# A transformer block, forward and backward, on one core: q and k of two chunks turned token-major by DMA, the first chunk's FFN in two token halves, its residual added by TensorE, and a new order

## The chip, the core and the metric

The kernel runs on one core of a Trainium2 chip. What is measured is the device time of one execution in microseconds (us); each kernel is run several times and the median is used. Before the change the three runs took 554.25, 555.15 and 555.99 us, so the median is 555.15. Beside these there is one execution under the hardware profiler, from which every row in this text comes. Engines are named as in the profile: PE is TensorE's matmul stream, PEld its weight loads, DVE is VectorE, ACT is ScalarE, POOL is GpSimd, SP is SyncE, which here does nothing but issue DMAs.

## The reference

A pre-norm block with a local attention and an FFN; the kernel returns the block's output and, for a given grad_out, the gradients of x, wqkv, wo, w1, b1, w2 and b2. Batch 1, S = 2048 tokens, D = 512, F = 1792, 32 heads of 16, window of 8 with a step of 2 back in time; inputs and outputs are bf16.

```python
def _A_ref(x, wqkv, wo):
    B, S, D = x.shape
    H = 32; Dh = D // H
    W, dil = 8, 2
    qkv = (lambda x, *d: x.transpose(*d))((x @ wqkv).reshape(B, S, 3, H, Dh), 2, 0, 3, 1, 4)
    q, k, v = qkv[0], qkv[1], qkv[2]
    pos = jnp.arange(S)
    off = jnp.arange(W) * dil
    idx = pos[:, None] - off[None, :]
    ...
    logits = jnp.einsum("bhsd,bhswd->bhsw", q, kg) * scale
    logits = jnp.where(mask[None, None, :, :], logits, -1e9)
    attn = _softmax(logits, axis=-1)
    o = jnp.einsum("bhsw,bhswd->bhsd", attn, vg)
    return (lambda x, *d: x.transpose(*d))(o, 0, 2, 1, 3).reshape(B, S, D) @ wo

def _B_ref(x, w1, b1, w2, b2):
    h = jnp.einsum("bsd,df->bsf", x, w1) + b1
    h = _gelu(h)
    return jnp.einsum("bsf,fd->bsd", h, w2) + b2

x = A_x
h = x + _A_ref(_layernorm(x, axis=-1), A_wqkv, A_wo)
h2 = h + _B_ref(_layernorm(h, axis=-1), B_w1, B_b1, B_w2, B_b2)
return h2
```

The outputs are h2 and, by jax.vjp, the seven gradients.

## The kernel before

The tokens are worked on in four chunks of 512, each of four tiles of 128 tokens. Per chunk the forward pass has the first layernorm; q and k as feature-major tiles (kt, qt: features on partitions, tokens along them) and v as a token-major one (tokens on partitions); attention, whose windowed products VectorE makes (prf, prbo) and TensorE sums over features with a 0/1 matrix; the product with wo and the residual (h); the second layernorm; its transposed copy ln2T; the FFN's first product and the gelu; and the second product, which gives h2. The backward pass follows chunk by chunk, and then the weight gradients, which run over all tokens.

Nothing is issued as it is written down. Every step is an op of a plan (L84), with its engine and what it reads and writes; a hand-given table, ORDER, says in which order the ops are emitted (L118 to L156), and thereby the program order of each engine, and a second table, HOMES, gives each buffer its place in SBUF or PSUM. Each engine goes through its program strictly in order, so an instruction that waits holds up all that stand behind it. Most DMAs are issued by SP, in order too; the gathers of the window (L471, 2304 KB each) by POOL, and a few stores by ACT. DMAs take their semaphores from eight lanes in turn, and one that takes a lane waits until the DMA eight places before it has landed.

What the change touches:

- **Token-major k and q.** The backward pass gathers windows of k and q from DRAM, token-major (k_d, q_d). p1_qkv decides at its end how they get there. Before the change all four chunks use to_tm_store: for each half chunk eight PE transposes (L434), one eviction of 128x1024 by ACT into tmk or tmq (L297) and one store of 256 KB (L287). The functions fm_store and tm_late also exist, but the table TML that selects them is empty: the first stores the feature-major tile to DRAM (kf_d, qf_d), the second loads it back through a transposing DMA (L291) into tmlk or tmlq and stores that to k_d or q_d.
- **The residual.** p1_h makes the product with wo in a PSUM tile, four matmuls for each tile of 128 tokens, and VectorE adds x (xp) out of SBUF while evicting (L747). Then come BN_STATS and BN_AGGR for each tile, and in layernorm, for four tiles at a time, ve (L371), a power on POOL (L373) and nm (L376); ACT applies them (L381) into ln_0, and to_fm_tiles transposes ln_0 on PE (L416) and has ACT evict ln2T.
- **The FFN's first product.** p2_h makes 14 PSUM tiles per chunk, each four matmuls of 512 columns, ACT adds the bias while evicting (xb, L774), and a gelu follows for each group of up to four (L777).
- **mmul** (L264 to L270) issues a product whole (L270) or, where its neighbours in the order use 32-column groups, as four 32-column pieces (L268), which TensorE streams beside each other.

Other names that come up: w1T is w1 loaded by a transposing DMA for the backward FFN; ro, ln1b and gw1in are loads from DRAM for the weight gradients; wgs and wgso are evicted weight gradients and their stores; gqkvT is a transposed gradient copied by ACT.

Of the kernel before, what the change touches and what calls it, by code (L numbers as in the profile page):

```python
# [10 lines left out]
P = 128  # L11
BF16 = mybir.dt.bfloat16
F32 = mybir.dt.float32
ACT = mybir.ActivationFunctionType
# [145 lines left out]
def kernel(  # L160
# [568 lines left out]
    def p1_h(c):  # L729
# [5 lines left out]
        for j in range(TPC):  # L735
            ps = ps_("psw", 1)

            def mm(j=j, ps=ps):
                for k in range(DC):
                    mmul(ps(), oT()[:, j, k * P:(k + 1) * P], wo()[:, k, :], start=(k == 0), stop=(not RESPE and k == DC - 1))  # L740
                if RESPE:
                    T.matmul(ps(), lhsT=ident[:], rhs=xt()[:, j, :], start=False, stop=True)
            op("PE", (5 if RESPE else 4) * MM, mm, r=[(oT, None if c in FMO else j // 2), wo] + ([xt, IDENT] if RESPE else []), w=[ps], tag="wo", cls=4)
            if RESPE:
                evict(h, lambda j=j: h()[:, j, :], ps, lambda ps=ps: ps(), 512, key=j, tag="h")
            else:
                op("DVE", tt_us(512, True), lambda j=j, ps=ps: V.tensor_tensor(out=h()[:, j, :], in0=ps(), in1=xt()[:, j, :], op=ALU.add),  # L747
                   r=[ps, xt], w=[(h, j)], tag="h")
        ln2 = sb("ln2_%d" % c, [P, TPC, D])
        layernorm(c, h, MV2, ST2, VE2, NM2, R2, mv2, st2, ve2, nm2, rstd2, ln2, N2[c], "2")  # L750
# [8 lines left out]
    def p2_h(c):  # L759
        d = st_[c]  # L760
        d["g"], d["d"] = [], []
        for b, (f0, f1) in enumerate(FB):
            n = f1 - f0
            N = n * 512
            xb = sb("xb", [P, n, 512])
            gl = sb("gl", [P, n, 512])
            for f in range(f0, f1):
# [407 lines left out]
TML = ()  # L1175
# [3 lines left out]
RESPE = False  # L1179
# [150 lines left out]
```

## Time and profile before

| | |
|---|---|
| median of three runs | 555.15 us |
| the profiled execution's own time | 557.15 us |
| its span, first to last instruction | 555.4 us |
| granted TensorE clock, mean | 0.999 |
| bytes moved by DMA | 126.40 MB |
| idle gaps of PE in front of chunk 0's FFN, 62 to 76 us | 1.78 us in three waits |
| evictions L297 of tmk and tmq, 16 | 16.1 us of ACT |
| residual additions L747, 16 | 10.8 us of DVE |
| bias evictions L774, 56 | 35.7 us of ACT |

The profile's span is 1.75 us shorter than the execution's time, and the profiled execution is 2.0 us longer than the median of the runs. In the rows below, a group's row reads: line, engine, operation, output and input names, shape and type, count, then busy us and the mean ns of one, then the idle time of that engine just before and what ended it. In a timeline row the first number is the start in us from the span's start, the second the length; square brackets give the idle time before and what ended it. A slice's digit is the busy share in tenths.

### The profile page before, as it was taken

Reading aid. Unit: us, or ns where it says so; the run is one execution under the profiler, and the core shown is the slowest. Engines: PE = TensorE matmul, PEld = TensorE weight load, DVE = VectorE, ACT = ScalarE, POOL = GpSimd, SP = SyncE. Lnnn points to the kernel's source line nnn. Section 1 sums busy time; section 2 is a strip of 40 time slices with the busy share of each in tenths; the row PEclk is TensorE's granted clock in tenths of the full one; section 3 lists DMA queues with packets and bytes.
Section 4 is the critical chain, followed back from the end, with each engine's and each line's share of the span. In section 5 each row is a group of like instructions: output and inputs, shape, how many; then the busy total and the mean of one; then the engine's idle time right before and its main releaser. Section 6 shows DMA issues by size and latency. Waiting matters only on the chain. (4 is left out here: it accounts for less than half of the span.)

```text
span 555.4 us, 13067 instructions
## 1 busy us (share of the span) xinstructions
PE 539.7 (97%) x5568; PEld 268.9 (48%) x5568; DVE 494.2 (89%) x648; ACT 324.2 (58%) x503; POOL 32.4 (6%) x38
## 2 busy tenths in 40 slices
PE   7999999999999999999999999999999998999995
PEld 4655554444444444444444444455455554555442
DVE  7999999999999999889885877789879998999992
ACT  4998699887999794996131324042324556633531
POOL 1610100021001000000000000000010001000000
PEclk9999999999999999999999999999999999999999
DMA  8898998975499617298999989999999999778237
GB/s 265 218 289 251 395 368 236 199 228 185 97 268 281 179 34 167 77 152 221 199 210 184 194 183 187 295 212 271 240 357 374 305 335 372 318 272 162 52 72 199
DMA packets 195306, 126.40 MB, mean 228 GB/s; under 512 B 149744, under 2 KB 190896, under 8 KB 193200
## 3 DMA queue, kind: packets, MB, share of 16 engines
q1 hardware_dynamic: 189760, 82.06, 64.5%
q0 software_dynamic: 3312, 41.42, 19.2%
q10 hardware_dynamic: 2176, 2.10, 1.2%
q8 instruction: 43, 0.70, 0.5%
q14 instruction: 15, 0.12, 0.1%
HBM read 55.74 MB, written 35.21 MB: 164 GB/s over the span
## 5 line engine op out<-in xcount | busy, mean ns | idle before, releaser
L270 PE MATMUL ps<-goT,w2T 128*128 128x512 bf16 x224 | 53.6, 379 | 0.8 <-DVE h2s L828 0.5
L270 PE MATMUL ps<-w1T,xb 128*128 128x512 bf16 x224 | 52.9, 379 | 0.0
L270 PE MATMUL ps<-w,gl 128*128 128x512 bf16 x216 | 50.5, 379 | 0.0
L297 ACT CAST wgs<-ps 128x512 bf16<-128x512 f32 (+1 forms) x30 | 16.2, 558 | 57.4 <-PE ps L268 35.7
L270 PE MATMUL ps<-ln2T,w 128*128 128x512 bf16 x188 | 44.2, 379 | 0.7 <-DVE xb L856 0.3
L774 ACT ACTIVATE xb<-ps,b1c 128x512 bf16<-128x512 f32 x56 | 35.7, 692 | 12.8 <-PE ps L270 12.5
L856 DVE SCALAR_TENSOR_TENSOR xb<-xb,ps 128x512 bf16<-128x512 bf16 x56 | 36.6, 685 | 6.2 <-PE ps L270 5.6
L518 DVE TENSOR_TENSOR prbq<-Rq,cfq 128x4096 bf16<-128x4096 bf16 x16 | 36.0, 2288 | 5.0 <-PE ps L487 1.7
L479 DVE TENSOR_TENSOR prb<-got,vw 128x4096 bf16<-128x4096 bf16 x16 | 36.3, 2282 | 2.7 <-PE ps L487 1.4
L518 DVE TENSOR_TENSOR prbv<-Rv,cfv 128x4096 bf16<-128x4096 bf16 x16 | 36.1, 2283 | 2.7 <-PE ps L268 1.8
L518 DVE TENSOR_TENSOR prbk<-Rk,cfk 128x4096 bf16<-128x4096 bf16 x16 | 36.1, 2283 | 0.7 <-PE ps L527 0.7
L518 DVE TENSOR_TENSOR prbo<-Ro,cfo 128x4096 bf16<-128x4096 bf16 x16 | 35.9, 2288 | 0.4 <-DMA k_d<-tmk 0.2
L479 DVE TENSOR_TENSOR prf<-qt,kt 128x4096 bf16<-128x4096 bf16 x16 | 35.5, 2275 | 0.0
L270 PEld LDWEIGHTS <-w2T 128*128 128x128 bf16 x224 | 21.8, 98 | 27.4 <-issue 2.0
L270 PEld LDWEIGHTS <-xb 128*128 128x128 bf16 x224 | 21.9, 98 | 26.4
L270 PEld LDWEIGHTS <-gl 128*128 128x128 bf16 x216 | 20.8, 98 | 25.6 <-issue 1.6
L796 ACT ACTIVATE xb<-xb 128x2048 bf16<-128x2048 bf16 (+1 forms) x16 | 26.8, 1690 | 7.8 <-DVE xb L795 7.7
L626 PE MATMUL ps<-ln1T,wqk 128*32 128x512 bf16 x512 | 30.2, 383 | 0.0
L270 PEld LDWEIGHTS <-w 128*128 128x128 bf16 x188 | 18.1, 97 | 23.0 <-issue 2.5
L268 PE MATMUL ps<-wqkvT,gqkvT 128*32 128x512 bf16 x448 | 27.4, 379 | 1.7 <-ACT gqkvT L297 1.6
L777 ACT ACTIVATE gl<-xb 128x2048 bf16<-128x2048 bf16 (+1 forms) x16 | 26.8, 1697 | 0.0
L792 ACT ACTIVATE x<-xb 128x2048 bf16<-128x2048 bf16 (+1 forms) x16 | 26.6, 1690 | 0.0
(198 smaller groups left out, 1054.0 us busy)
## 6 DMA issues: line engine op xcount, KB each, us to landing
Ro<-v_d POOLq DMA_DIRECT2D x4, 2304.0 KB, 11.2
Rq<-k_d POOLq DMA_DIRECT2D x4, 2304.0 KB, 11.6
Rv<-go_d POOLq DMA_DIRECT2D x4, 2304.0 KB, 14.2
Rk<-q_d POOLq DMA_DIRECT2D x4, 2304.0 KB, 13.4
g_d<-gl SPq DMA_DIRECT2D x9, 512.0 KB, 3.5
gh_d<-xb SPq DMA_DIRECT2D x9, 512.0 KB, 3.4
w<-in_B_w_dram SPq DMA_DIRECT2D x2, 1792.0 KB, 15.0
out_dram<-wgs SPq DMA_DIRECT2D x13, 256.0 KB, 7.1
```

Of the source, the lines that this page charges most:

```text
L268: T.matmul(out[32 * a:32 * a + 32, :], lhsT=l[:, 32 * a:32 * a + 32], rhs=r, start=start, stop=stop, skip_group_check=True)
L270: T.matmul(out, lhsT=l, rhs=r, start=start, stop=stop, skip_group_check=True)
L297: fn = lambda: A.copy(out=ap(), in_=pap())
L479: op("DVE", tt_us(4096), lambda g=g, pr=pr: V.tensor_tensor(out=pr(), in0=ql()[:, g, :].unsqueeze(1).to_broadcast([P, W, 512]), in1=_sub(k ...
L518: V.tensor_tensor(out=pr().rearrange("p a j (d h) -> p a j d h", h=H), in0=_sub(R()[:, o0, 0:1], [[st, 2], [512, 4], [32, DH], [1, H]]), i ...
L626: T.matmul(ps()[32 * a:32 * a + 32, gg * 512:(gg + 1) * 512], lhsT=_sub(wq_()[:, dc, 0:1], [[DH, H]], sel * D + 4 * g + a), rhs=rhs, start ...
L774: op("ACT", act_us(512, 1), lambda f=f, ps=ps, xb=xb, f0=f0: A.activation(out=xb()[:, f - f0, :], in_=ps(), func=ACT.Identity, bias=b1c[:, ...
L777: op("ACT", act_us(N), lambda xb=xb, gl=gl: A.activation(out=fl(gl), in_=fl(xb), func=ACT.Gelu_apprx_tanh), r=[xb], w=[gl], tag="gelu", mo ...
L792: op("ACT", act_us(N), lambda xb=xb, x2=x2: A.activation(out=fl(x2), in_=fl(xb), func=ACT.Square), r=[xb], w=[x2], tag="x2")
L796: op("ACT", act_us(N), lambda xb=xb: A.activation(out=fl(xb), in_=fl(xb), func=ACT.Tanh, scale=GC), w=[xb], tag="tanh", mode=6)
L856: op("DVE", 0.61, lambda f=f, ps=ps, z=z, f0=f0: V.scalar_tensor_tensor(out=z()[:, f - f0, :], in0=z()[:, f - f0, :], scalar=1.0, in1=ps() ...
```

## The change

It does four things.

1. TML now names k and q of chunks 2 and 3. For these to_tm_store (16 transposes, two ACT copies and two stores each) is replaced by fm_store and tm_late: a 512 KB store, a 512 KB transposing load and a 512 KB store, all three issued by SP.
2. RESPE names chunk 0: its residual comes from one more matmul per tile, the identity against x, in the same PSUM accumulation, and ACT casts the sum into h (L297) where VectorE added it (L747).
3. HALVES names chunk 0: its FFN's first product runs over two halves of 256 tokens, each 14 groups of four matmuls of 256 columns and 14 bias evictions of 128x256; a half needs only two of the four tiles of ln2T. The second layernorm of that chunk takes its tiles in groups of two.
4. ORDER and HOMES are new throughout.

```diff
                 for k in range(DC):
-                    mmul(ps(), oT()[:, j, k * P:(k + 1) * P], wo()[:, k, :], start=(k == 0), stop=(not RESPE and k == DC - 1))
-                if RESPE:
-                    T.matmul(ps(), lhsT=ident[:], rhs=xt()[:, j, :], start=False, stop=True)
...
-            if RESPE:
+                    mmul(ps(), oT()[:, j, k * P:(k + 1) * P], wo()[:, k, :], start=(k == 0), stop=(c not in RESPE and k == DC - 1))
+                if c in RESPE:
+                    mmul(ps(), ident[:], xt()[:, j, :], start=False, stop=True)
...
+            if c in RESPE:
                 evict(h, lambda j=j: h()[:, j, :], ps, lambda ps=ps: ps(), 512, key=j, tag="h")
...
-        layernorm(c, h, MV2, ST2, VE2, NM2, R2, mv2, st2, ve2, nm2, rstd2, ln2, N2[c], "2")
+        layernorm(c, h, MV2, ST2, VE2, NM2, R2, mv2, st2, ve2, nm2, rstd2, ln2, N2[c], "2", per=2 if c in HALVES else TPC)
...
+        xbs = [sb("xb", [P, f1 - f0, 512]) for f0, f1 in FB] if c in HALVES else ()
+        for f, hh in [(f, hh) for hh in range(2) for f in range(FT)] if c in HALVES else ():
+            ps, xb, i, o = ps_("psi", 1), xbs[f // 4], f % 4, 256 * hh
+
+            def mmh(f=f, ps=ps, o=o):
+                for dc in range(DC):
+                    mmul(ps()[:, 0:256], w1()[:, dc, f * P:(f + 1) * P], cols(ln2T[c], dc, False)[:, o:o + 256], start=(dc == 0), stop=(dc == DC - 1))
+            op("PE", 4 * MM / 2, mmh, r=[w1, (ln2T[c], 2 * hh), (ln2T[c], 2 * hh + 1)], w=[ps], tag="ff1", cls=4)
+            op("ACT", act_us(256, 1), lambda f=f, ps=ps, xb=xb, i=i, o=o: A.activation(out=xb()[:, i, o:o + 256], in_=ps()[:, 0:256], func=ACT.Identity,
+                                                                                   bias=b1c[:, f:f + 1]), r=[ps, B1C], w=[(xb, (f, hh))], tag="xb")
...
-TML = ()
+TML = tuple((n, c) for n in "kq" for c in (2, 3))
...
-RESPE = False
+RESPE = (0,)
+HALVES = (0,)
...
 ORDER = (
-    8, 22, 0, 11, 12, 23, 1, 7, 10, 6, 9, 48, 364, 27, 13, 49, 50, 26, 51, 44, 61, 28, 2, 62, 40, 25, 3, 45, 29, 41, 24, 46, 52, 42, 43, 53, 363, 15,
+    8, 10, 0, 65, 6, 21, 12, 14, 7, 27, 48, 9, 26, 49, 15, 50, 25, 11, 19, 51, 18, 40, 28, 44, 41, 1, 2, 3, 4, 29, 5, 42, 43, 52, 45, 61, 36, 24, 17,
...
```

In the changed file the lines below p2_h lie ten further on (the bias eviction of the halves is L770, r_d's and rst's lines go from L1114 and L1117 to L1124 and L1127); the helpers' lines are the same.

How the new order moves instructions is shown at three places. The numbers within a name are those of one buffer, and say nothing else. First SP, from the transposing loads of normalised tiles (ln2T) to the loads of w1T; r_d, rst and xp are small loads and stores, g_d, gh_d and out_dram stores of results. Before:

```order
L291 DMA_TRANSPOSE ln2T_478_34_1913<-ln_2_465_34_1879 128x16x128
L287 DMA k_d<-tmk_23_538 128x2x512
L1114 DMA r_d<-rtr 16x32
L291 DMA_TRANSPOSE ln2T_533_38_2030<-ln_1_520_37_2003 128x16x128
L287 DMA g_d_73<-gl_27_1688 128x4x512
L1117 DMA rst<-r_d 32x4x16
L287 DMA out_dram<-h2s_35_1915 128x1x512
L1117 DMA rst<-r_d 32x4x16
L287 DMA gh_d_77<-xb_28_1394 128x4x512
L291 DMA_TRANSPOSE w1T_41_2268<-in_B_w_dram 128x14x128 x2
```

Now:

```order
L291 DMA_TRANSPOSE ln2T_535_39_2098<-ln_1_520_38_2067 128x16x128
L287 DMA g_d_73<-gl_31_1805 128x2x512
L291 DMA_TRANSPOSE tmlk_42_2121<-kf_d_91 128x4x512
L287 DMA q_d<-tmlq_32_1886 128x4x512
L287 DMA out_dram<-h2s_36_2034 128x1x512
L282 DMA xp_415_29_1702<-in_A_x_dram 32x4x512
L287 DMA k_d<-tmlk_42_2121 128x4x512
L291 DMA_TRANSPOSE tmlq_41_2240<-qf_d_86 128x4x512
L287 DMA q_d<-tmlq_41_2240 128x4x512
L287 DMA out_dram<-h2s_36_2034 128x1x512
L287 DMA g_d_73<-gl_32_1816 128x4x512
L1084 DMA k_d<-zrow 16x512
```

The next row there is the pair of w1T loads. Two transposing loads and three 512 KB stores of k and q have come in; the store of tmlq into q_d stands directly behind the load that fills tmlq, and w1T behind both.

Second, ACT from the last casts before chunk 0's FFN into that FFN. ln_0 and ln2T are the normalised tiles and their transposed copy, xb the bias evictions, ost the attention output of the next chunk. Before:

```order
L297 COPY ln2T_303_25_1293<-ps 128x4x128 x2
L297 CAST qt_293_20_1246<-ps 128x1024
L297 COPY tmk_28_1380<-ps 128x1024
L297 COPY tmk_29_1386<-ps 128x1024
L774 ACTIVATE xb_28_1394<-ps,b1c 128x512 x2
L532 ACTIVATE ost_27_1431<-ps 128x512 x2
L774 ACTIVATE xb_28_1460<-ps,b1c 128x512
L532 ACTIVATE ost_27_1431<-ps 128x512
L297 COPY tmq_29_1475<-ps 128x1024
L532 ACTIVATE ost_27_1431<-ps 128x512
L297 COPY oT_355_30_1493<-ps 128x1024
```

Now:

```order
L297 CAST qt_311_24_1375<-ps 128x1024
L532 ACTIVATE ost_29_1416<-ps 128x512
L297 COPY ln2T_314_26_1389<-ps 128x4x128 x2
L532 ACTIVATE ost_29_1416<-ps 128x512
L770 ACTIVATE xb_28_1450<-ps,b1c 128x256
L770 ACTIVATE xb_29_1456<-ps,b1c 128x256
L770 ACTIVATE xb_30_1466<-ps,b1c 128x256
L297 COPY oT_345_32_1474<-ps 128x1024
L770 ACTIVATE xb_30_1466<-ps,b1c 128x256
L532 ACTIVATE ost_29_1416<-ps 128x512
L770 ACTIVATE xb_29_1456<-ps,b1c 128x256 x2
```

The copies of tmk and tmq are gone from between the bias evictions, and these are of 256 columns.

Third, SP in the late stage, where the loads of ro and ln1b for the last weight gradients stand among the stores of wgs. Before:

```order
L282 DMA ro_1474_36_4943<-o_d_71 128x2048
L287 DMA out_dram<-wgs_1492_37_5032 128x2x512
L287 DMA out_dram<-wgs_1403_38_4568 128x2x256
L282 DMA ln1b_34_5284<-ln_d_62 32x4x512
L282 DMA ln1b_31_5422<-ln_d_64 32x4x512
L287 DMA out_dram<-wgs_1533_34_5360 128x2x512
L282 DMA ro_1556_32_5451<-o_d_72 128x2048
L282 DMA ln1b_33_5453<-ln_d_61 32x4x512
L282 DMA ln1b_31_5422<-ln_d_64 32x4x512
```

Now:

```order
L282 DMA ro_1483_41_5265<-o_d_71 128x2048
L287 DMA out_dram<-wgs_1363_41_4682 128x2x512
L287 DMA out_dram<-wgs_1418_42_4845 128x2x256
L287 DMA out_dram<-wgs_1366_39_4689 128x2x512
L287 DMA out_dram<-wgs_1462_40_5140 128x2x512
L287 DMA out_dram<-wgs_1510_40_5339 128x2x512
L282 DMA ln1b_32_5654<-ln_d_64 32x4x512
L282 DMA ln1b_34_5675<-ln_d_63 32x4x512 x2
```

Before, a ro load stood among the ln1b loads; now all ro loads stand ahead of the first of them, with five stores of wgs between.

More of the change, by code (lines that the diff above doesn't have):

```diff
@@ L739, in mm @@
                 for k in range(DC):
-                    mmul(ps(), oT()[:, j, k * P:(k + 1) * P], wo()[:, k, :], start=(k == 0), stop=(not RESPE and k == DC - 1))
-                if RESPE:
-                    T.matmul(ps(), lhsT=ident[:], rhs=xt()[:, j, :], start=False, stop=True)
-            op("PE", (5 if RESPE else 4) * MM, mm, r=[(oT, None if c in FMO else j // 2), wo] + ([xt, IDENT] if RESPE else []), w=[ps], tag="wo", cls=4)
-            if RESPE:
+                    mmul(ps(), oT()[:, j, k * P:(k + 1) * P], wo()[:, k, :], start=(k == 0), stop=(c not in RESPE and k == DC - 1))
+                if c in RESPE:
+                    mmul(ps(), ident[:], xt()[:, j, :], start=False, stop=True)
+            op("PE", (5 if c in RESPE else 4) * MM, mm, r=[(oT, None if c in FMO else j // 2), wo] + ([xt, IDENT] if c in RESPE else []), w=[ps], tag="wo", cls=4)
+            if c in RESPE:
                 evict(h, lambda j=j: h()[:, j, :], ps, lambda ps=ps: ps(), 512, key=j, tag="h")
@@ L764, in p2_h @@
             N = n * 512
-            xb = sb("xb", [P, n, 512])
+            xb = xbs[b] if c in HALVES else sb("xb", [P, n, 512])
             gl = sb("gl", [P, n, 512])
-            for f in range(f0, f1):
+            for f in range(f0, f1) if c not in HALVES else ():
                 ps = ps_("psh", 1)
```

203 rows, old and new, of tables (HOMES, ORDER) are left out of this document.

## The prediction

> **What bounds the kernel now.** I read the page's busy shares first, then its forty slices, then a table by stage, and only then single waits.
>
> ```profile
> PE 539.7 (97%) x5568; PEld 268.9 (48%) x5568; DVE 494.2 (89%) x648; ACT 324.2 (58%) x503; POOL 32.4 (6%) x38
> ```
>
> TensorE is busy 539.7 of 555.4 us: all idle time together is under 16 us, and by the slices, of 13.9 us each, a good part of that lies at the start and the end:
>
> ```profile
> PE   7999999999999999999999999999999998999995
> ...
> DVE  7999999999999999889885877789879998999992
> ...
> DMA  8898998975499617298999989999999999778237
> ```
>
> So the time is the matmul stream plus few gaps, and what leaves the stream is worth its full length wherever no other engine takes over as the bound. VectorE could: its digits are 9 from the second slice to the sixteenth, about 14 to 222 us, the stretch in which every edit of this change but the order lies. The table by 15 us shows how close the three engines are where the edits are:
>
> ```profile
> 60.00:75.00 15.00, 13.22 (x187) 7.77 (x185) 14.69 (x24) 11.19 (x14) 1.03 (x1) 1.00 1.00 392
> 75.00:90.00 15.00, 14.98 (x154) 8.16 (x153) 14.83 (x8) 14.39 (x23) 0.60 (x1) 1.00 0.91 286
> 90.00:105.00 15.00, 14.39 (x186) 6.69 (x185) 14.65 (x12) 14.24 (x16) 0.00 (x0) 1.00 0.86 242
> ```
>
> The columns are start and end, length, busy us of PE, PEld, DVE, ACT and POOL, granted clock, DMA share and GB/s. From 75 to 105 us PE has 29.4 of 30 us, DVE 29.5 and ACT 28.6: whoever gets more work there decides. The granted clock is 1.00 in each of these, so no term below is scaled by it.
>
> **TensorE's sum.** Four pairs (k and q of chunks 2 and 3) lose their 16 transposes each.
>
> ```profile
> 76.61 1.12 PE L434 MATMUL ps<-ident,kt 128*128 128x128 bf16 x16
> 77.61 2.75 PE L270 MATMUL ps<-ln2T,w 128*128 128x512 bf16 x12
> ```
>
> The next group starts 1.00 us after the 16 transposes of L434 began, so a group of 16 is worth 1.00 us of the stream and the four pairs 4.0 us. Other eights stand in the chain at 0.45 us, which would make it 3.6. I take 3.8. The residual of chunk 0 adds one identity matmul of 512 columns to each of four products:
>
> ```profile
> 477.15 0.86 PE ps L270 x4
> ```
>
> 0.86 us for four, so +0.9. The halves make 112 matmuls of 256 columns of 56 of 512. Two timeline rows give the spacing of 256 columns, one chain row that of 512 in the four-column-group form, and one row how fast its weights load:
>
> ```profile
> 371.37 2.78 PE L270 MATMUL ps<-gw1in,ln 128*128 128x256 bf16 x24
> 373.99 0.60 PE L270 MATMUL ps<-xw1in,ln 128*128 128x256 bf16 x4
> ```
> ```profile
> 422.30 2.59 PE ps L268 x48
> ```
> ```profile
> 455.08 0.12 PEld L527 LDWEIGHTS <-S 128*32 128x32 bf16 x8
> ```
>
> 24 take 2.62 us, 109 ns each against 0.86/4 = 215 ns for 512 columns: two halves cost 3 ns more than a whole, 0.2 us over 56 pairs. The built program issues 20 of the 112 in the form of four 32-column pieces. At 512 columns a piece takes 2.59/48 = 54 ns, and no row shows it at 256: 27 ns if the stream rules, 54 if the issue does, so +0 to +2.2 us over 80 pieces. Eight 32-column weight loads in 0.12 us say that four of them fit into 107 ns, so I take 0 and keep 2.2 for the range. Sum of TensorE: −3.8 + 0.9 + 0.2 = **−2.7 us**.
>
> The Trainium skill, "TensorE: Matmul & The Clock Gate", section "Back-to-back issue gap", speaks against the halves: it gives about 131 ns a matmul sustained at 512 columns and 81 ns at 128. By it (98 ns at 256 columns by a straight line, an estimate from that page) a pair of halves would cost 64 ns more than a whole and the 56 pairs 3.6 us, and the sum would be +0.7 instead of −2.7. The rows above, 109 ns against 215, speak against it.
>
> **VectorE**, which must fall too if TensorE's gain is to reach the end:
>
> ```profile
> L747 DVE TENSOR_TENSOR h<-ps,xp 128x512 bf16<-128x512 f32 x16 | 10.8, 674 | 0.4 <-issue 0.2 <-PE ps L270 0.2
> ...
> L371 DVE TENSOR_SCALAR ve<-mv 128x4 f32<-128x4 f32 x7 | 1.2, 169 | 0.2
> ```
> ```profile
> L376 DVE SCALAR_TENSOR_TENSOR nm<-mv,rstd 128x4 f32<-128x4 f32 x7 | 1.1, 154 | 1.6 <-POOL rstd L373 1.6
> ```
>
> Four additions of 0.674 go; the layernorm of chunk 0 in two groups adds one L371 and one L376: −2.70 + 0.32 = **−2.4 us**, and all of it ahead of chunk 0's FFN. That is nearly TensorE's gain, so the bound of the first 220 us falls by 2.4 to 2.7 and not by TensorE's part alone. The second rstd on POOL (L373) stands beside an engine that is 6% busy.
>
> **ScalarE.** What goes are eight copies, four of tmk and four of tmq in the same form:
>
> ```profile
> L297 ACT COPY tmk<-ps 128x1024 bf16<-128x1024 bf16 x8 | 8.1, 1028 | 0.3 <-PE ps L434 0.3
> ```
>
> 8 × 1.03 = −8.2. What comes are four evictions of h, cast from 512 columns like these:
>
> ```profile
> L297 ACT CAST wgs<-ps 128x512 bf16<-128x512 f32 x26 | 14.8, 587 | 50.8 <-PE ps L268 35.7 <-PE ps L270 14.9
> ```
>
> 4 × 0.587 = +2.3. And of the 14 bias evictions of chunk 0 come 28 of half the length, which no row shows; beside the whole one stands the cast of 256 columns:
>
> ```profile
> L774 ACT ACTIVATE xb<-ps,b1c 128x512 bf16<-128x512 f32 x56 | 35.7, 692 | 12.8 <-PE ps L270 12.5 <-PE ps L268 0.2
> ...
> L297 ACT CAST wgs<-ps 128x256 bf16<-128x256 f32 x4 | 1.4, 372 | 6.6 <-PE ps L270 6.6
> ```
>
> The 14 take 9.7 us. From above, 692 ns for a half (nothing saved by halving): 28 × 0.692 − 9.7 = +9.7; from below, 372: +0.7. By the step between the two casts, 587 − 372 = 215 ns, a half takes 692 − 215 = 477 ns, my value, since it is the same step of columns out of the same memory: +3.7. Sum **−2.2 us**, with bounds −5.2 and +3.8. It lands well: about four of the removed copies (chunk 3's, 4.1 us) lie between 78 and 88 us, in the stretch where ACT has 28.6 of 30, and the four casts come before it, where ACT has 11.2 of 15.
>
> **DMA and the queues.** Each of the four pairs now makes a 512 KB store, a 512 KB transposed load and a 512 KB store of what made two 256 KB stores, all on SP. The nearest transposed load:
>
> ```profile
> L291 SPq DMA_TRANSPOSE vw<-v_d x4: 2045/2576/3145, 259.6 to 342.3; - x4
> ```
>
> Its issue keeps SP 2.6 us, and the same view has how long the data take:
>
> ```profile
> DMA to landing us min/median/max: 5.0/5.9/6.6
> ```
>
> So each of the four costs SP 2.6 us, and the data are there 5.9 us later. The store of q waits for that landing, and in one place the program has it right behind its own load, so SP stands still up to 5.9 us with the w1T loads behind it. What there is of slack:
>
> ```profile
> 135.48 0.58 SPq L1117 DMA_DIRECT2D rst<-r_d  x1
> 145.35 0.40 SPq L287 DMA_DIRECT2D gh_d<-xb  x1
> ```
> ```profile
> 156.12 2.81 SPq L291 DMA_TRANSPOSE w1T<-in_B_w_dram  x1
> ```
> ```profile
> 164.29 1.03 PE L270 MATMUL ps<-w1T,xb 128*128 128x512 bf16 x4
> ```
>
> SP issues nothing from 136.1 to 145.3 us, 9.2 us, which covers two issues of 2.6 and most of one landing. On the other side the last w1T issue ends at 158.9 and its first user starts at 164.3. I cost this at nothing, covered by those 9 us; if the cover is gone the price is in a rival below. The 4 MB more that move fall about 100 to 150 us, where the DMA digits are 7, 5 and 4: by them some 19 us of all queues' time lie open. Nobody reads these tensors soon:
>
> ```profile
> L471 POOL DMA_DIRECT2D Rq<-k_d x4: 527/530/600, 348.8 to 458.2; - x4
> ```
>
> **The order.** It is rewritten as a whole, so its waits must be counted as unknown. The gaps which may go are these:
>
> ```profile
> 74.54 0.38 PE L416 MATMUL ps<-ident,ln 128*128 128x128 bf16 x4 [1.03 <-ACT kt L297]
> ```
> ```profile
> 458.37 0.43 ACTq L287 DMA_DIRECT2D out_dram<-wgso  x1
> 458.85 1.93 ACT L297 COPY gqkvT<-ps 128x1024 bf16<-128x1024 bf16 x2 [3.46 <-DMA ln1b<-ln_d]
> ...
> 459.91 2.77 PE L268 MATMUL ps<-wqkvT,gqkvT 128*32 128x512 bf16 x48 [1.62 <-ACT gqkvT L297]
> ```
> ```profile
> 439.54 18.76 DMA ln1b<-ln_d
> ```
>
> The first lies before chunk 0's FFN, where the halves need only two of the four normalised tiles: up to 1.0 us. The second: ACT's store of wgso waits until an ln1b load has landed, which took 18.8 us among the gathers; the copy of gqkvT behind it on ACT is late by 3.5 us, and TensorE by 1.6. In the new order the last ro load and five wgs stores stand ahead of the ln1b loads, so this meeting is likely to change, though the same kind of wait can come up at another place. Bounds of the order: −2.6 if both go and nothing comes, and +2.6 if as much as that comes anew, since no row can show a wait that isn't there yet. I take 0.
>
> **Sum.** −2.7 us on TensorE, carried by VectorE's −2.4 and ScalarE's −2.2 in the same stretch: the span of 555.4 becomes 552.7. Around it lay 1.75 us (the profiled execution took 557.15), so that execution would be 554.45; the median of the runs is 555.15, 2.0 below the profiled one, so **552.4 us** for the runs.
>
> **Rivals.**
>
> *The order gives it back (about 555).* The saving opens gaps: TensorE reaches its next consumer 2.7 us earlier and waits there for VectorE, which has 14.7 of 15 in most early windows, or for a transfer. For it: VectorE saves only ahead of chunk 0's FFN, while half of the transposes leave later. Against: PE is at 15.00 of 15 in nearly all later windows. Less than 1.6 of the 2.7 us are left: 553.5 to 555.5.
>
> *Halves dearer on TensorE (about 554.6).* If the 80 pieces take 54 ns each, as pieces of 512 columns do, the 2.2 us left out above come back: 552.4 + 2.2. For it: no row shows a piece spaced closer. Against: eight weight loads of that form in 0.12 us. The section of the Trainium skill named above would make the halves dearer still, by its 3.6 us in place of the 0.2 (555.8, an estimate); the trace's 109 ns disagrees.
>
> *More goes than leaves (about 549.8).* Both waits above vanish: 552.4 − 2.6.
>
> *ScalarE becomes the bound, 75 to 105 us (about 558).* If a half eviction costs close to a whole, ACT gets +9.7 and loses 4.1 there, 5.6 us more against 1.4 idle: it ends 4.2 us late, and the gelu behind it too. Chunk 2's transposes, 1.9 us, went earlier, and the residual's 0.9 came: 555.15 + 4.2 − 1.9 + 0.9 = 558.4. It decides from 28x − 9.7 − 4.1 − 1.4 = 1.0, that is x = 0.58 us a half; the step between the casts makes 0.48. So it needs 100 ns more than I see.
>
> *SP late for w1T (about 559.9).* Two issues of 2.6 and one landing of 5.9 make 11.1 us against 9.2 idle and 0.4 of slack (158.9 + 5.0, a landing as quick as the quickest vw load, against 164.3): 1.5 us short, which the issues of tmk that are gone and products of other kinds cover. With the second landing in front of w1T too, it is 7.4 us short: 555.15 − 2.7 + 7.4 = 559.9. It decides from 2.7 us short on, that is with a fifth of the second landing.
>
> **How the numbers follow.** Forecast 0.43, more goes 0.16: together faster by over 0.3% (1.67 us, about what a measurement of this kernel can tell from no change), 0.59. Given back 0.15 and dearer halves 0.08: within 0.3%, 0.23. ScalarE 0.08 and SP 0.10: slower, 0.18. The forecast's own range is 551 to 553.5. The range that holds 8 in 10 takes in the larger gain at 549.8, a little more at that end for the bounds of ScalarE (549.0), and goes to 558.0 at the other: the 2.2 us of the pieces, the 2.6 of the order and the cheaper part of both slower cases; the rest of these, about 0.12, and what lies below 549 are left out.
>
> **What would show it.** Right: 64 instead of 128 transposes at L434, VectorE's L747 at 12, the windows from 45 to 105 us shorter by about 2.5 us together, PE busy near 537. Half evictions near 480 ns: ScalarE rival out; above 580: in. The start of the first w1T product shows SP: no later than 164 less the gain, or the rival holds. The wait for gqkvT shows the order's part. The 256-column pieces at 27 or 54 ns show the term I put at 0. The forecast is wrong if TensorE's idle grows by more than its busy time falls.

## The result, and the profile after

| | before | after |
|---|---|---|
| median of the runs | 555.57 us (4 runs) | 564.55 us (4 runs) |
| ratio, 95% interval | | 1.0167 [1.0135, 1.0198] |
| profiled execution, its span | 557.15, 555.4 us | 563.26, 561.5 us |
| granted clock, mean | 0.999 | 0.994 |
| idle waits of PE, summed | 9.4 us in 15 | 15.9 us in 20 |

The changed kernel is 9.0 us slower, and outside the predicted range. Here and below, medians are over all executions, while ratios leave out those that were disturbed, longer and at a lower granted clock.

The page of after, its busy shares and four of its slices:

```profile
PE 539.3 (96%) x5705; PEld 275.7 (49%) x5705; DVE 492.8 (88%) x646; ACT 321.1 (57%) x513; POOL 24.9 (4%) x39
...
PE   8999999999999999999999989999994999999996
...
DVE  7989999999999799999786667977829999999984
...
PEclk9999999999999999999999999999997999999999
```

TensorE's busy time is 0.4 us less than before, its waits are 6.5 us more, and 6.5 − 0.4 is the 6.1 us between the spans. By the slices the loss is in one place: the 31st, where PE shows 4, the clock shows 7, and VectorE shows 2 in the slice before. The table by stage has that place in us; its columns are those of the prediction. Before:

```profile
405.00:420.00 15.00, 15.00 (x288) 8.21 (x280) 12.43 (x11) 3.67 (x9) 1.48 (x3) 1.00 0.97 370
420.00:435.00 15.00, 15.00 (x232) 8.36 (x228) 15.00 (x8) 9.35 (x15) 0.54 (x1) 1.00 0.91 338
```

After:

```profile
405.00:420.00 15.00, 15.00 (x206) 7.05 (x208) 2.89 (x4) 3.76 (x9) 0.94 (x3) 1.00 0.98 339
420.00:435.00 15.00, 7.96 (x63) 3.54 (x56) 14.91 (x11) 3.11 (x7) 1.38 (x3) 0.77 0.91 351
```

VectorE stops first (409.4 us), TensorE some 12 us later (421.4). The waits of after, with the total, the count and the longest one in us, say for what:

```profile
POOL Rk L471 <- DMA out_dram<-wgs: 14.1, 1, 14.1
DVE cfk L497 <- DMA out_dram<-wgs: 10.4, 1, 10.4
```
```profile
PE ps L527 <- DVE prbq L518: 7.0, 1, 7.0
PE ps L270 <- DVE xb L866: 1.7, 5, 0.5
PE ps L268 <- DMA ghT<-ghr: 1.5, 1, 1.5
```

Nobody reads these stores of wgs. What waits for them is whoever writes next to the same place in SBUF. HOMES puts cfk (a transposed piece of an attention gradient, L497) where one of the wgs tiles had been, and the tile must have left before cfk may be written. The timelines of POOL, SP and VectorE, in that order:

```profile
404.68 0.53 POOL L471 DMA_DIRECT2D Rq<-k_d  x1 [27.89 <-DVE prbv L518]
```
```profile
399.77 4.45 SPq L291 DMA_TRANSPOSE gw1in<-gh_d  x1
...
405.41 7.36 SPq L287 DMA_DIRECT2D out_dram<-wgs  x5
```
```profile
419.80 1.14 DVE L497 STREAM_TRANSPOSE cfk<-glf 128x512 bf16<-128x512 bf16 x1 [10.43 <-DMA out_dram<-wgs]
420.86 2.11 DVE L497 STREAM_TRANSPOSE cfq<-glf 128x512 bf16<-128x512 bf16 x2
...
426.11 8.90 DVE L518 TENSOR_TENSOR prbq<-Rq,cfq 128x4096 bf16<-128x4096 bf16 x4
```

At 404.68 POOL issues a gather of 2304 KB. From 405.41 on SP issues the five stores of wgs that the third place of the new order shows, right behind it. The tile in cfk's place has been complete since 362 us, but its store is the third of the five. It lands at 419.7, and only then does VectorE write cfk. cfk itself isn't urgent, but VectorE works in order: cfq and prbq stand behind it, and TensorE's sum at L527 waits for prbq. Before, the same tile's store went out at 388.68, ahead of the gather:

```profile
388.68 2.23 SPq L287 DMA_DIRECT2D out_dram<-wgs  x1
```

The DMA view of 404 to 421 us (KB each, median us to landing), and SP's view of all 15 such stores, after:

```profile
Rq<-k_d POOLq DMA_DIRECT2D x1, 2304.0 KB, 12.0
...
out_dram<-wgs SPq DMA_DIRECT2D x5, 256.0 KB, 10.3
```
```profile
DMA to landing us min/median/max: 2.1/4.5/13.2
```

The gather lands at about 416.7, and half of the five stores take 10.3 us or more. Ours, issued at 406.45, takes 13.2, the longest way of all fifteen. What exactly holds it up isn't shown: beside the gather, the load of gw1in and smaller transfers are under way, and the DMA share of these 15 us is 0.98.

The gap has a tail on TensorE. Three timeline rows and three windows of 4 us, after:

```profile
418.66 2.76 PE L268 MATMUL ps<-gw1in,ln 128*32 128x512 bf16 x48
428.46 1.05 PE L527 MATMUL ps<-prbq,S 128*32 128x512 bf16 x8 [7.04 <-DVE prbq L518]
...
435.27 0.61 PE L543 MATMUL ps<-ident,gqs 128*128 128x128 bf16 x8
...
436.70 0.61 PE L527 MATMUL ps<-prbq,S 128*32 128x512 bf16 x8
437.14 2.76 PE L268 MATMUL ps<-ghr,ro 128*32 128x512 bf16 x48
```
```profile
424.00:428.00 4.00, 0.00 (x0) 0.00 (x0) 3.91 (x3) 0.00 (x0) 0.00 (x0) 0.60 0.98 403
428.00:432.00 4.00, 3.54 (x21) 1.67 (x22) 4.00 (x3) 0.00 (x0) 0.00 (x0) 0.54 1.15 415
432.00:436.00 4.00, 4.00 (x30) 2.20 (x29) 4.00 (x3) 2.68 (x6) 0.53 (x1) 1.00 0.52 209
```

The clock falls in the gap and comes back some 3 us after work resumes (0.54 in the window from 428 us, 1.00 from 432 on). The next group starts 0.98 us after the eight sums of L527 at 428.46, but 0.44 us after the same eight at 436.70.

### The profile page after: what moved, and what is told of

It reads as the page before. It is cut to its first block, busy times and chain, and to the rows that moved or that the text cites. A ratio compares the mean times of both kernels' runs of the same rounds, so it can differ in the third digit from the quotient of the medians.

```text
span 561.5 us, 13345 instructions
## 1 busy us (share of the span) xinstructions
PE 539.3 (96%) x5705; PEld 275.7 (49%) x5705; DVE 492.8 (88%) x646; ACT 321.1 (57%) x513; POOL 24.9 (4%) x39
## 5 line engine op out<-in xcount | busy, mean ns | idle before, releaser
L270 PE MATMUL ps<-goT,w2T 128*128 128x512 bf16 x204 | 49.7, 379 | 1.4 <-DVE xb L866 1.1
L297 ACT CAST wgs<-ps 128x512 bf16<-128x512 f32 (+1 forms) x30 | 16.0, 558 | 59.9 <-PE ps L268 30.7
L270 PE MATMUL ps<-w,gl 128*128 128x512 bf16 x206 | 47.7, 379 | 0.6 <-DVE h L747 0.6
L270 PE MATMUL ps<-ln2T,w 128*128 128x512 bf16 (+1 forms) x228 | 43.8, 336 | 0.6 <-ACT xb L784 0.3
L270 PE MATMUL ps<-w1T,xb 128*128 128x512 bf16 x182 | 41.7, 379 | 0.5 <-DVE xb L866 0.5
L479 DVE TENSOR_TENSOR prf<-qt,kt 128x4096 bf16<-128x4096 bf16 x16 | 35.7, 2280 | 0.8 <-ACT kt L297 0.8
L270 PEld LDWEIGHTS <-w2T 128*128 128x128 bf16 x204 | 19.9, 98 | 26.1 <-issue 2.8
L784 ACT ACTIVATE xb<-ps,b1c 128x512 bf16<-128x512 f32 x42 | 27.2, 690 | 7.9 <-PE ps L270 7.6
L270 PEld LDWEIGHTS <-w 128*128 128x128 bf16 x228 | 21.7, 97 | 19.8 <-issue 3.5
L270 PEld LDWEIGHTS <-xb 128*128 128x128 bf16 x182 | 17.7, 98 | 22.2 <-issue 0.8
L270 PE MATMUL ps<-gor,gw2in 128*128 128x512 bf16 x104 | 24.9, 379 | 0.0
## 6 DMA issues: line engine op xcount, KB each, us to landing
Rq<-k_d POOLq DMA_DIRECT2D x4, 2304.0 KB, 11.1
```

What stands on the lines that cost most here:

```text
L270: T.matmul(out, lhsT=l, rhs=r, start=start, stop=stop, skip_group_check=True)
L297: fn = lambda: A.copy(out=ap(), in_=pap())
L479: op("DVE", tt_us(4096), lambda g=g, pr=pr: V.tensor_tensor(out=pr(), in0=ql()[:, g, :].unsqueeze(1).to_broadcast([P, W, 512]), in1=_sub(k ...
L784: op("ACT", act_us(512, 1), lambda f=f, ps=ps, xb=xb, f0=f0: A.activation(out=xb()[:, f - f0, :], in_=ps(), func=ACT.Identity, bias=b1c[:, ...
```

## The experiments

The theory **T**: the landing of that one store, issued behind the gather, makes VectorE late and TensorE with it. The rivals: **C**, most of the loss is the lowered clock; **G**, without any collision the new order would still be no faster; **D**, one of the three other parts (DMA turns, residual, halves) is slow by itself. Each run was measured beside runs of the kernel before, whose medians were 555.8 to 556.4 us; a ratio is to these.

**Two ways to take the wait for cfk away.** f1 issues the store earlier, on SP:

```diff
-L291 DMA_TRANSPOSE gw1in_39_5220<-gh_d_79 128x4x512
+L287 DMA out_dram<-wgs_1366_39_4689 128x2x512
+L291 DMA_TRANSPOSE gw1in_38_5221<-gh_d_79 128x4x512
 L287 DMA out_dram<-wgs_1437_44_4961 128x2x512
 ...
-L287 DMA out_dram<-wgs_1366_39_4689 128x2x512
```

> The changed kernel with one row of its order moved: on SP the store of one wgs tile (the one whose place in SBUF cfk of chunk 1 takes over) stands ahead of the transposing gw1in load that waits until 399.8 us, so it is issued near 398 instead of 406.5 us, before the Rq gather of 404.7. Nothing else changes. Theory A (one collision of places: VectorE's first write of cfk waits 10.4 us for that store's landing, TensorE then 7.0 us for VectorE, and runs at a lower clock for some us after it): the wait of cfk is gone, TensorE has no gap over 1 us near 421, the span is 561.5 - 7.2 - 1.4 = 552.9, the time about 555.5 (554.5 to 556.5). Theory B (the gather itself lands too late, since 4 MB more are moved and the DMA queues are full): prbq then waits for Rq instead, and less than 3 us come back, time over 561. Theory C (the parts of the change cost it, early): the stretch up to 300 us is longer, the time stays over 559.

f2 leaves the stores alone and moves both writes of cfk on VectorE behind the first two prbq:

```diff
-L497 STREAM_TRANSPOSE cfk_39_5333<-glf_47_4377 128x4x128
 ...
+L518 TENSOR_TENSOR prbq_36_5506<-Rq_39_5304,cfq_36_5367 128x4096
+L497 STREAM_TRANSPOSE cfk_37_5508<-glf_47_4377 128x4x128 x2
```

> The changed kernel with two rows of VectorE's order moved: both writes of cfk of chunk 1 stand behind the first two products prbq of that chunk instead of ahead of four other transposes and of those products. The store of wgs and all places stay. Theory A: the store lands as late as before (near 419.8), but nothing urgent waits behind it: TensorE has no gap over 1 us near 421, time within 1 us of the kernel with the early store. Theory B: no gain over 3 us.

Measured: f1 558.68 us, 1.0060 [1.0033, 1.0086]; f2 559.57 us, 1.0063 [1.0039, 1.0087]. Two different edits, one of a store and one of its victim, each take out the gap at 421 and win 5 to 6 us. f1 still misses its expected 554.5 to 556.5. In both kernels the next meeting of the same kind shows: POOL waits 14.3 us (f2: 14.4) for other wgs stores, in whose places it gathers Rk, and TensorE 2.4 us (f2: 4.0) for the products of that gather (POOL's timeline, then TensorE's waits, f1):

```profile
422.02 0.53 POOL L471 DMA_DIRECT2D Rk<-q_d  x1 [14.32 <-DMA out_dram<-wgs]
```
```profile
PE ps L527 <- DVE prbk L518: 2.4, 1, 2.4
```

**The clock's share.** f3 keeps the wait and fills it with work whose result is thrown away: 120 more products of the identity with itself into the bank that the waiting sum then starts anew.

```diff
+            for _ in range(120 if pl.cur == 1314 else 0):
+                T.matmul(ps()[:, 0:P], lhsT=ident[:], rhs=ident[:], start=True, stop=True, skip_group_check=True)
```

> The changed kernel with 120 identity matmuls of 128 columns put on TensorE right ahead of the sum that waits for prbq, into that sum's own PSUM bank, which it then overwrites: the wait stays, but TensorE is not idle in most of it. If the lower granted clock after the gap costs 1.4 us, the granted clock of 420 to 435 us is 1.00 instead of 0.77 and the time falls by 1 to 1.6 us, to about 563; if that clock costs nothing, the time stays at 564.5.

The same kernel was run a second time:

> A second look at the changed kernel with 120 identity matmuls in the wait, since the first profile fell into a disturbed run. If the gap costs clock: granted clock 1.00 from 420 to 435 us where the changed kernel has 0.77, and a span 1 to 1.6 us below 561.5; if not, the span stays.

Measured: 564.37 us, 1.0143 [1.0116, 1.0169], and 563.88 us, 1.0142 [1.0110, 1.0174]. The second run's window:

```profile
420.00:435.00 15.00, 14.30 (x200) 10.26 (x189) 14.09 (x10) 3.84 (x9) 1.59 (x3) 1.00 0.89 334
```

The clock stays at 1.00, and the stretch from the sum of prbq to the next group of L543 with gqs takes 5.3 us (429.48 to 434.80) instead of 6.8 (428.46 to 435.27). So the lowered clock costs 1.5 us at that place. More than half of it is lost again at once, since TensorE then waits 0.62 us for prbk: the stretch began 1.02 us later than in after, and the next 16 products of ghr start 0.34 us later (440.94 against 440.60), so 0.7 us is left. In the whole time nothing of it shows, although 1 to 1.6 us were expected: the interval overlaps that of after, and the span is 561.6. C is at most the smaller part of 9 us.

**The collision planted where there was none.** p1 takes the kernel of before, moves the same tile's store from 388.7 us to behind the gather of Rq, and the first write of cfk next to the second:

```diff
-L287 DMA out_dram<-wgs_1338_43_4341 128x2x512
-L282 DMA ro_1397_40_4557<-o_d_69 128x2048
+L282 DMA ro_1396_41_4556<-o_d_69 128x2048
 ...
 L282 DMA ro_1472_36_4940<-o_d_71 128x2048
+L287 DMA out_dram<-wgs_1338_43_4341 128x2x512
```

> The kernel before, with none of the change in it, but with the suspected collision planted by two moves in its order: SP's store of the wgs tile whose place cfk of chunk 1 takes over goes from 388.7 us to behind the Rq gather (404.0), and VectorE's first write of cfk from 394.8 to 410.2 us, right ahead of the other cfk write. Theory A (a store caught behind the 2304 KB gather, and a tile that takes its place early in VectorE's order): VectorE waits 6 to 10 us at about 410 us, TensorE runs dry between 410 and 425, the time rises by 4 to 9 us, to 559.5 to 565. Rival (the wait is peculiar to the changed kernel, its greater DMA load or its shorter supply of matmuls): less than 2 us.

p0 is its control, with only cfk moved:

> The kernel before with only the second of these moves (VectorE's first write of cfk at 410.2 instead of 394.8 us), the store left at 388.7. Theory A: no wait for a store, the time within 1 us of the kernel before. If the move itself is dear (1.1 us of VectorE more in front of prbq): up to 1.5 us above.

Measured: p1 575.25 us, 1.0331 [1.0293, 1.0368]; p0 557.09 us, 1.0022 [0.9987, 1.0056]. VectorE's timeline and TensorE's waits, p1:

```profile
429.86 2.15 DVE L497 STREAM_TRANSPOSE cfk<-glf 128x512 bf16<-128x512 bf16 x2 [18.13 <-DMA out_dram<-wgs]
```
```profile
PE ps L527 <- DVE prbq L518: 15.9, 1, 15.9
```

The same wait at the same line, in a kernel with none of the other edits: T is shown in both directions. In p0 nothing waits for cfk's place; only one short wait for another wgs store came, 1.9 us of VectorE ahead of prbq, where none was expected. The price was missed: 17 us over the control by the ratios, instead of 4 to 9. POOL's timeline of p1 has three gathers around that store, which SP issues at 406.21:

```profile
404.53 0.53 POOL L471 DMA_DIRECT2D Rq<-k_d  x1 [25.80 <-ACT sr L297]
406.41 0.53 POOL L471 DMA_DIRECT2D Rk<-q_d  x1 [1.35 <-DMA out_dram<-wgs]
...
409.44 0.53 POOL L471 DMA_DIRECT2D Rv<-go_d  x1 [1.98 <-PE ps L527]
```

The store took 23.6 us to land. In after only Rq was under way, since Rk was itself held up until 419.80. That the two further gathers make the difference is read from these rows; no run leaves them out.

**All of it cleared.** f4 moves four of the stores ahead of the load of gw1in:

> The changed kernel with four rows of SP's order moved: the stores of the four wgs tiles whose places cfk and Rk of chunk 1 take over all stand ahead of the transposing gw1in load, so they are issued before the Rq gather instead of behind it. With one of them moved, cfk's wait of 10.4 us was gone, but POOL still waited 14.3 us for the other stores before it could issue the Rk gather (422.0 us), and TensorE stood 2.6 us at 433 for prbk with a granted clock of 0.89 behind it. Theory A (all of the loss is this collision of places with stores caught behind a gather): Rk is issued before 415 us, no gap over 1 us stands between 410 and 440, the time falls by another 3 to 4.5 us to 554 to 555.7, that is 0 to 2 us below the kernel before. Rival (the rest of the loss is elsewhere, in the parts or in other waits of the new order): the time stays at 557.5 to 559.

Measured: 565.74 us as the median of 12, in two groups: five of 555.8 to 562.4, for which the ratio of 1.0018 [0.9981, 1.0056] stands, and seven of 565.6 to 576.3, of which the profile is one. SP's timeline and TensorE's:

```profile
399.10 4.08 SPq L287 DMA_DIRECT2D out_dram<-wgs  x5
403.23 4.84 SPq L291 DMA_TRANSPOSE gw1in<-gh_d  x1
```
```profile
420.38 4.89 PE L268 MATMUL ps<-gw1in,ln 128*32 128x512 bf16 x44 [8.16 <-DMA gw1in<-gh_d]
```

The four stores push the load of gw1in from 399.77 to 403.23, up against the gather (404.96 in this run), and now TensorE waits 8.2 us for the load. None of the five faster runs has a profile, but h1 (below), with the same rows of SP and without halves, has one of 554.45 us. There the load goes out at 401.80, as close ahead of the gather (403.56), and costs 0.7 us (TensorE's timeline, h1):

```profile
411.50 4.50 PE L268 MATMUL ps<-gw1in,ln 128*32 128x512 bf16 x80 [0.69 <-DMA gw1in<-gh_d]
```

So the same rows of SP can meet or miss. That the five faster runs missed is likely; what decides it isn't shown. f5 moves two stores to about 391 us and two more ahead of the ro loads, and these loads behind gw1in:

```diff
 L291 DMA_TRANSPOSE tmgod_42_4847<-got_42_4828 128x16x128
+L287 DMA out_dram<-wgs_1366_39_4689 128x2x512
+L287 DMA out_dram<-wgs_1363_41_4682 128x2x512
 L287 DMA out_dram<-wgs_1415_42_4838 128x2x256
 ...
+L287 DMA out_dram<-wgs_1439_42_4963 128x2x512
+L287 DMA out_dram<-wgs_1418_42_4845 128x2x256
```

> The changed kernel with only SP's order mended around the Rq gather near 405 us: the stores of two wgs tiles stand at 391 us (their data is there since 362), those of two others ahead of two ro loads, and these two loads, which are used from 437 us on, stand behind the transposing gw1in load. So all four places are free before cfk and Rk are written, and the gw1in load, which in the kernel with four early stores was issued 3.4 us later (403.2) and whose first user then waited 8.2 us, is issued no later than before. Theory A (DMAs caught behind the gather are all that is lost): no gap over 1 us between 405 and 440, 553.5 to 555.5 in most runs, 1 to 2.5 us below the kernel before. Rival (the 2.6 us that left TensorE's stream come back as idle time in other places of the new order): 555.5 to 556.5, the same as before.

Measured: 557.16 us, 1.0030 [1.0006, 1.0053]. Windows and waits of TensorE, f5:

```profile
405.00:420.00 15.00, 14.95 (x201) 7.22 (x203) 12.90 (x12) 3.32 (x7) 1.59 (x3) 1.00 1.01 387
420.00:435.00 15.00, 14.95 (x215) 8.03 (x212) 13.23 (x7) 9.39 (x16) 1.59 (x3) 1.00 1.02 408
```
```profile
PE ps L270 <- DVE xb L866: 1.7, 5, 0.5
...
PE ps L268 <- DMA ghT<-ghr: 1.2, 1, 1.2
PE ps L527 <- DVE prbk L518: 1.1, 1, 1.1
PE ps L527 <- DVE prbv L518: 0.8, 1, 0.8
```

TensorE's stream is whole again at this place and 7.4 us of the 9.0 are back, but the kernel is still not faster than before, and above both of the ranges written for it: T explains the loss, and G what is left. TensorE's waits sum to 11.1 us in f5. In three profiles of kernels in before's order they sum to 9.4 (before), 8.5 (p0) and 7.3 (bR, below); that is 1.7 to 3.8 us less. For before the row of xb at the same place is this:

```profile
PE ps L270 <- DVE xb L856: 0.6, 3, 0.2
```

What left the stream is 2.9 us by h1's page (below, without halves) and 1.9 by that of after; f5's own page lacks 35 of 5705 matmul records and can't tell. So most of it came back as small waits. This is read from rows; no run took these waits away one by one.

**The parts by themselves.** h1 is f4, and g5 is f5, with chunk 0's FFN whole again:

```diff
-HALVES = (0,)
+HALVES = ()
```

> The kernel with the four early stores, chunk 0's first FFN product whole again (14 products of 512 columns at every second place of the 28 halves; the second layernorm still in groups of two tiles). TensorE stays within 0.3 us, ScalarE falls by 28 x 0.47 - 14 x 0.69 = 3.5 us. If ScalarE's longer evictions cost the change anything between 75 and 105 us, the time falls by 1 to 3 us; if the halves help by starting on two of four tiles, TensorE waits before the FFN grow by 0.5 to 2 us and the time rises by as much; if neither, it stays within 0.8 us.

> The kernel of f5_all_clear with chunk 0's first FFN product whole again, at every second place of the halves; the second layernorm still in groups of two tiles. TensorE +-0.3 us, ScalarE -3.5 us. One look at the same edit on the kernel with four early stores gave a span of 552.7 us, with TensorE's waits from 75 to 90 us 0.7 us longer and those from 90 to 120 us 1.2 us shorter than with halves. So within 0.8 us of f5_all_clear, if anything below it; if the halves carry the change, 1 us or more above it.

Measured: h1 554.45, 556.86, 571.69 and 583.79 us, too few and too far apart for a ratio; g5 556.71 us, 1.0004 [0.9965, 1.0042] against f5's 1.0030 [1.0006, 1.0053]. The intervals overlap: the halves neither cost nor bring what these runs could tell. h1's page gives the stream without them:

```profile
PE 536.8 (97%) x5613; PEld 271.2 (49%) x5613; DVE 492.8 (89%) x646; ACT 319.2 (58%) x499; POOL 24.9 (4%) x39
```

r1 is f1 with the residual back on VectorE, bR is before with only the residual on TensorE:

```diff
-RESPE = (0,)
+RESPE = ()
```

> The kernel with the early store, with chunk 0's residual added by VectorE again (RESPE empty; same order, same places): TensorE -0.9 us, ScalarE -2.3, VectorE +2.7. If VectorE bounds the first 220 us, the time is 1 to 2 us above the kernel with the early store; if TensorE does, 0 to 0.9 below it.

> The kernel before with only chunk 0's residual on TensorE and ScalarE (RESPE = (0,)), order and places as before. TensorE +0.9 us, VectorE -2.7, ScalarE +2.3. If VectorE bounds the first 220 us, 1 to 2.5 us below the kernel before; if TensorE does, 0 to 0.9 above it; if ScalarE's casts are late in its queue, more.

Measured: r1 563.18 us, 1.0142 [1.0099, 1.0186], against f1's 1.0060; bR 557.08 us, 1.0027 [0.9996, 1.0058]. The window of 60 to 90 us, f1 and then r1:

```profile
60.00:90.00 30.00, 29.04 (x390) 19.07 (x381) 29.70 (x31) 24.49 (x43) 1.99 (x3) 1.00 0.99 368
```
```profile
60.00:90.00 30.00, 26.13 (x354) 17.07 (x348) 29.63 (x34) 20.27 (x36) 1.99 (x3) 1.00 0.97 359
```

In the new order, with the four additions on VectorE, TensorE is 2.9 us less busy in that stretch. A part of this is work that r1 doesn't have, the identity products; the stream itself falls 2.2 us behind (the group of 24 halves' products that starts at 87.18 in f1 starts at 89.40 in r1). The medians differ by 4.5 us, where 1 to 2 were expected, and the profiled spans (560.2 and 558.8) by 1.4 only; where the rest comes from isn't shown. In the old order taking the additions away brought nothing that could be measured. So the edit's worth depends on the order, and a trial in the other order tells little of it.

The turn by DMA couldn't be isolated. bT is before with only TML set, tU is f5 with TML empty, in both with the new ops put into the order by hand:

> The kernel before with only the first part of the change: k and q of chunks 2 and 3 go through a 512 KB store, a transposing load and a 512 KB store in place of 64 transposes, 8 copies and 8 stores; order and places as before, the twelve DMAs put at fitting places of SP. TensorE -3.8 us, ScalarE -8.2. If TensorE's sum reaches the end: 2.5 to 4 us below the kernel before. If VectorE bounds the first 220 us: within 1.2 us of it. If SP's standing still is dear (w1T late): above it.

> The kernel of f5_all_clear with the first part undone: k and q of chunks 2 and 3 are turned by 64 transposes on TensorE, 8 copies on ScalarE and 8 stores again, put right behind the products that make them, at 47 to 49 and 70 to 76 us; all else in the order of f5_all_clear. TensorE +3.8 us, ScalarE +8.2. If TensorE's sum reaches the end: 2.5 to 4.5 us above f5_all_clear. If VectorE bounds the first 220 us and hides it: within 1.2 us. Rival: without the large DMAs on SP it is faster.

Measured: bT 576.21 us, 1.0263 [1.0218, 1.0308]; tU 571.94 us, 1.0271 [1.0228, 1.0314]. One has the turn and one hasn't, and both are slower by the same 2.6 to 2.7%. What they have in common is ops placed by hand, which may be the cause; neither tells what the turn costs or brings. Of D, then: no loss by the halves could be told, the residual's part is a gain in this order, and the turn by DMA stays open.

## Why the prediction was wrong, point by point

Its own sign of being wrong came: TensorE's idle time grew by 6.5 us and its busy time fell by 0.4.

- **TensorE's sum, −2.7: right in its parts.** L434 has 64 transposes where 128 were. h1, which has the first two terms alone, stands at 536.8 against 539.7, 2.9 less, as −3.8 + 0.9 has it. For the pieces of 256 columns, put at 0 with 2.2 as the bound, after shows 48 in 1.31 us, 27 ns each, so "halves dearer" is out as priced there:

```profile
81.15 1.48 PE L268 MATMUL ps<-ln2T,w 128*32 128x256 bf16 x48
82.46 0.60 PE L527 MATMUL ps<-prbo,S 128*32 128x512 bf16 x8
```

  After's 539.3 holds 1.5 us of lowered clock; without it the stream fell by 1.9. The 0.8 short of the sum weren't followed up.
- **VectorE, −2.4: 1.0 too much.** 494.2 became 492.8, −1.4. The four additions did go (L747 now 8.0 us in 12), and what came instead is spread over many rows by 0.1 to 0.3 each.
- **ScalarE, −2.2: right within its bounds.** 324.2 became 321.1, −3.1. A half eviction takes 481 ns where 477 were estimated, so the rival of ScalarE as the bound is out. But counts times mean durations overstate the busy time, since the evictions overlap: the 28 halves keep ScalarE busy for 11.2 us and the 14 wholes that went for 8.5 (35.7 to 27.2), so +2.7 where the sum had +3.7:

```profile
L770 ACT ACTIVATE xb<-ps,b1c 128x256 bf16<-128x256 f32 x28 | 11.2, 481 | 0.3 <-PE ps L270 0.2
```

- **SP and the turns by DMA, 0: no loss seen, but not isolated.** The loads of tmlq landed within 5.9 us. The first product with w1T starts at 169.75, later than the 164 that was to speak against the rival of a late SP, so by that sign the rival would hold. But in the new order other products stand ahead of it, and it runs in a stream without a wait, so TensorE did not stand for w1T:

```profile
169.75 1.03 PE L270 MATMUL ps<-w1T,xb 128*128 128x512 bf16 x4
```

- **The order, "I take 0", bounds −2.6 to +2.6: the step that failed.** Its good half came true: neither the wait for kt at 74.5 nor that for gqkvT at 458 is among after's waits. Its bad half was bounded by the size of the gaps that were there ("as much as that comes anew"), and that is no bound for a new wait: one of 7.0 us came, from a store of wgs that held VectorE for 10.4, with 1.5 more of lowered clock. The cause stood in the text: five stores of wgs in new places on SP, and a landing that took 18.8 us among the gathers. The step drew from these only that another meeting "is likely to change". It didn't ask who writes next to the places of those five tiles, how early that writer stands on its engine, and what waits behind it. With the landing as the bound, 18.8 us less the slack of the users, the slower side would have had its mechanism, and the range would have reached much further up.
- **"The order gives it back": right as a second cause.** It stood at 0.15, at 553.5 to 555.5. By f5 it, and not the forecast, would have been the outcome without the collision, and at a worse place than named: 557.16 beside 555.77 for before, with an interval that begins 0.06% above before. The mechanism it named, small waits for VectorE or a transfer, fits f5's rows.

None of the versions is clearly faster than before.

## What to carry to other kernels

When an order moves a store or load past a large gather, look up its landing, not its issue: list the tiles that take over its place in SBUF, and see how early the first write to them stands on its in-order engine. A write that nobody needs soon can hold the one that everybody needs. Bound a wait that isn't there yet by the longest landing seen in that stretch less the user's slack, never by the gaps that happen to be there (p1's 23.6 us, beyond the 18.8 of the prediction, shows that even this can be too little); and expect the place that was cleared to pass the meeting on, as gw1in showed, until all that stands near the gather has been looked at.

## What the runs showed of the hardware

A store of wgs (128 or 256 KB) took 2.1 us from issue to landing at best; the one in cfk's place (256 KB) took 13.2 with one gather of 2304 KB under way, in after, and 23.6 with three, in p1.

A gap of TensorE of 2.40 us was enough to lower its clock. It stands in f1 (TensorE's timeline, then the window behind it):

```profile
435.98 0.80 PE L527 MATMUL ps<-prbk,S 128*32 128x512 bf16 x8 [2.40 <-DVE prbk L518]
```
```profile
436.00:440.00 4.00, 4.00 (x44) 1.69 (x48) 3.11 (x2) 0.00 (x0) 0.00 (x0) 0.57 1.08 440
```

The gap of 1.62 us that before has at 459.91 left no such mark, its clock is 1.00 from 405 to 470 us, and neither did one of 1.88 us that f2 has at 331.97, with 1.00 from 328 to 340. The Trainium skill, "TensorE: Matmul & The Clock Gate", section "Why this matters for your kernels", gives as the rule no idle gaps above some 3 us. The 7.04 us of after agree with it, at 0.60 and 0.54; the 2.40 us of f1 don't, and here the measurement decides. In no profile of this case did a gap of up to 1.88 us lower the clock, and in all of them each of 2.40 us or more did. That isn't a limit yet, for the clock doesn't follow the gap at once: by windows of 0.1 us it stands at 0.50 in f1 from 436.3 to 439.7, so it falls only when TensorE works again, and in after from 424.9 to 431.7, 3.4 us after the gap began. Once lowered, it stayed so for 3.4 us in f1 and for twice that in after.
